# Where the sines and the products kn, qn stand in a four-block cycle of attention under an MLP

## The chip, the cores and the metric

One core of a Trainium2 chip runs the whole program. The number is device microseconds of one execution, from the first to the last instruction and what the launch puts around them; lower is better. The engines are named as in the profile: PE (TensorE, the matrix engine), PEld (its weight loads), ACT (ScalarE, functions from tables), DVE (VectorE, elementwise), POOL (GpSimd), SP (SyncE, which here only issues DMAs).

## What is computed

A linear attention with a complex decay, followed by two MLP layers:

```python
for t in range(S):                       # S = 768, 4 batches, 8 heads, 48 wide
    S_re, S_im = ar * S_re - ai * S_im + kv, ar * S_im + ai * S_re
    y[:, :, t] = q[:, :, t] @ S_re       # (ar, ai): a_re, a_im scaled to at most 0.999
x = y as 3072 tokens of 384
h = x @ w_in;  x = (h - tanh(h)) @ w_out       # d_ff = 2048
h = x @ w_in2; x = (max(h, 0) ** 2) @ w_out2
```

The kernel uses no loop over t. The time axis is cut into 6 chunks of 128 steps; in a chunk, logarithms of the magnitudes and angles of a are summed by a triangular matmul, exponentials and sines of the sums turn q and k, and the decay becomes an ordinary masked product of the turned q and k.

## The kernel before

The MLP sets the pace. It is cut into blocks: one block is one group of 512 tokens and one slice of 128 of the 2048 hidden columns, with nine matmuls h (first weight, three k-slices with three products each of a number split in high and low halves) and nine matmuls acc (second weight). 17 blocks make the first group, 16 every other; there are 6 groups and 2 layers. The acc of a block stand two blocks behind its h. Between them ACT makes t = tanh(h), DVE the difference h - t, ACT the high half gh, DVE the low half gl (`act_parts`, line 284).

Attention is cut into units, 4 batches in each of 6 chunks; unit n has chunk c = n // 4 and batch b = n % 4. A unit is a list of steps 0 to 15 (lines 790 to 817), and each step is done in one block, four blocks apart from the same step of the next unit. So four units are in flight, and every fourth block is a visit: there stand step 15 of one unit, 11 of the next, 7 of the third, 3 of the fourth. From the second group on, while attention lasts, `chain["on"]` is true and every engine works in the order in which the code is written (class `Turn`, line 144); before and behind that a scheduler orders the instructions. In a block, the second number of a step is its key: keys are sorted, and `block_step` (line 1066) cuts them at 1.35, 1.75, 5, 6 and 7 to put the parts of the MLP between them. Keys under 5 stand before the block's h matmuls, the others behind them.

The steps in question, for a unit of chunk 2 or later:

- a0 loads ri (a_re, a_im, in three rotating buffers), a1 squares it on ACT into ab.
- a2 takes logarithms and exponentials (one table), a3 works on them on DVE, a3b splits ab into lh and ll.
- a6l sums on PE into pc, a7x takes the exponentials of pc into ee (the table of a2). a4 is the arctangent, a5c and a5s work on its result, a6 sums into pu, a7 makes the fraction of a turn in fg and sends its last row to DRAM (crow) for the next chunk.
- a8 takes the two sines of fg in place, a9 multiplies q and k by them into kn and qn (two DVE instructions each), t0 and t1 turn these over on PE into pk and pq, ACT copies them to kqT.
- In step 15: strips, pU, px on PE, wm on DVE; a12v copies px into the next group's tokens (xh, xl), a13v updates the state.

Functions of ACT come from tables, and `table(...)` (line 166) writes a load where the set in force lacks the function: logarithms and exponentials need one set, the arctangent a second (sigmoid), the sine a third (silu); tanh is in the second and the third. `ready(...)` is such a load ahead of time. PSUM has one bank for h in this part (`ps_tile`, line 86), so the next h waits until DVE has made h - t; pU, pu and pk share a second, px, pc and pq a third.

At a group's end `put_x2` (line 328) copies the three acc banks through tiles x2t to DRAM. The tag x2t has two buffers; with `third` the third copy takes a tile of another pool.

Of the kernel before, what the change touches and what calls it, by code (L numbers as in the profile page):

```python
# [43 lines left out]
def kernel(  # L44
# [10 lines left out]
    B, S, HV, DP = v.shape  # L55
# [86 lines left out]
    chain = {"on": False}  # L142
# [23 lines left out]
    def table(*names):  # L166
        if act_set["name"] not in names and not general[0]:
            name = names[0]
            with ExitStack() as es:
                for o in act_set["ops"] or [act_set["load"]]:  # L170
                    if o is not None:
                        es.enter_context(tc.issue_after(o))
                load = act_e.preload_act_table_set(name).ins
            act_set.update(name=name, load=load, ops=[])
# [138 lines left out]
    def g2(layer, m, g, acc, cs=slice(0, TG), js=range(KD)):  # L313
        gh, gl = g
        wh, wl = (w_[:, DM:] for w_ in wts[layer, m])
        first = m <= 0 and cs.start == 0
        end = m in (-1, NM - 1)
        for j in js:
            sl = slice(j * P, (j + 1) * P)
            o = acc[j][:, cs]  # L320
            ten.matmul(o, wh[:, sl], gh, start=first, stop=False)
            ten.matmul(o, wh[:, sl], gl, start=False, stop=False)
            ten.matmul(o, wl[:, sl], gh, start=False, stop=end)

    def new_acc():
        return [ps_c.tile([P, TG], F32, tag="c", name="acc") for _ in range(KD)]

    def put_x2(acc, dst, third=False):
        for j in range(KD):
            if third and j == 2:  # L330
                t = spool.tile([P, n2], F32, tag="cv", name="x2t")[:, :TG]
            else:
                t = gpool.tile([P, TG], F32, tag="x2t", name="x2t", bufs=2)
            if j % 2 == 0:
                act_e.copy(t, acc[j])
            else:
                dve.tensor_copy(t, acc[j])
            sp.dma_start(dst(j), t)
# [18 lines left out]
    def put_out(ap3, acc, g, j, cs=slice(0, TG), vector=False):  # L357
        t = ap3.tile([P, TG], F32, tag="ot", name="ot", bufs=3)
        if vector:
            dve.tensor_copy(t[:, cs], acc[j][:, cs])  # L360
        else:
            act_e.copy(t[:, cs], acc[j][:, cs])
        sp.dma_start(out[g, j * P:(j + 1) * P, cs], t[:, cs])
# [16 lines left out]
    at = [xpool.tile([P, 2, HH, P], F32, tag=g, name=f"at_{g}") for g in ("xh", "xl")]  # L380
# [16 lines left out]
    def unit(n):  # L397
        c, b = divmod(n, B)
# [225 lines left out]
        def a10(i):  # L624
            def pe():
                for src, nm in ((V["kn"], "pk"), (V["qn"], "pq")):
                    pt = bank(nm)
                    w = P if packed else D2
                    nt = n2 // w // 2
                    for j in range(nt):  # L630
                        ten.transpose(
                            pt[:w, j * P:(j + 1) * P],
                            src[:, (i * nt + j) * w:(i * nt + j + 1) * w], ident,
                        )
                    V[nm, i] = pt

            def ev():
                for dst, nm in (("kT", "pk"), ("qT", "pq")):
                    w, nt = (P, 3) if packed else (D2, HH)
                    act_e.copy(  # L640
                        T(dst, i)[:w, :nt].rearrange("p j t -> p (j t)"),
                        V[nm, i][:w, :nt * P],
                    )
                if packed:
                    for j in range(3):
                        sp.dma_start(
                            kqT[i][32 * j:32 * j + 32, :, 3, :], kqT[i][D2:P, :, j, :]
                        )

            return pe, ev  # L650

        def a11(half=range(2)):
            for i in half:
                sc = bank("sc").rearrange("p (j t) -> p j t", j=HH)
                for j in range(HH):
                    ten.matmul(
                        sc[:, j, :], head("kT", i * HH + j), head("qT", i * HH + j),
                        start=True, stop=True,
                    )
                V["sc", i] = sc  # L660
# [4 lines left out]
        def a11s(i):  # L665
            sc = strips[i]
            for j in (0, 2, 1, 3):
                h = i * HH + j
                for s in range(4):
                    g = 3 - s if turned(h) else s  # L670
                    ten.matmul(
                        sc[32 * g:32 * g + 32, j, 32 * s:],
                        head("kT", h)[:, 32 * s:32 * s + 32],
                        head("qT", h)[:, 32 * s:], start=True, stop=True,
                    )

        def a11m(i):
            sc = strips[i]
            wm = ap1.tile([P, HH, P], F32, tag=f"wm{i}", name=f"wm{i}_{n}")
            dve.tensor_tensor(  # L680
                wm.rearrange("p (a j) t -> p a j t", a=2),
                sc.rearrange("p (a j) t -> p a j t", a=2),
                maskab.unsqueeze(2).to_broadcast([P, 2, HH // 2, P]), op=ALU.mult,
            )
            V["wm", i] = wm
# [90 lines left out]
        t0, t0v = a10(0)  # L776
        t1_, t1v = a10(1)
        if c == 0:
# [3 lines left out]
                t0=t0, e0=t0v, t1=t1_, e1=t1v, s0=lambda: a11((0,)), s1=lambda: a11((1,)),  # L782
                m0=lambda: a11v((0,)), m1=lambda: a11v((1,)),
                px=a12, x=a12v, pU=a13, st=a13v, ff=fill,
            )
        def ready(name):
            if chain["on"]:
                table(name)

        if not packed:  # L790
            return [
                (i, dict(p=1, e=5.1, v=5.2, p2=6.1, v2=6.2)[kind], f) for i, kind, f in (
# [7 lines left out]
                )  # L800
            ]
        late = n - 2 * B
        ln = (2, 6.37) if late == 2 else (3, 1.4)
        ex = (6, 6.36) if late == 1 else (7, 1.3)
        at = (8, 6.05) if late == 1 else (7, 6.1)
        return [
            (0, 5.2, a0), (1, 5.2, a1), ln + (a2,), (3, 1.5, lambda: ready("sigmoid_and_others")),
            (4, 5.1, a3), (5, 5.1, a3b), (6, 6.3 if late < 2 else 1.1, a6l),
            (6, 1.4, a0c), ex + (a7x,), (7, 2.0, l2), at + (a4,), (at[0], 7.1, a5c),
            (8, 5.1, a7r), (9, 5.3, a5s), (9, 5.4, a8x),  # L810
            (10, 6.3 if late < 1 else 1.1, a6), (10, 6.4 if late < 1 else 1.2, a7),
            (10, 1.3, lambda: ready("silu_and_others")), (10, 6.5, a8),
            (11, 1.9, a9), (12, 5.2, l3), (12, 6.1, t0), (12, 6.2, t0v), (13, 6.1, t1_), (13, 6.2, t1v),
            (15, 1.1, lambda: a11s(0)), (15, 1.2, lambda: a11m(0)), (15, 1.5, a13),
            (15, 1.6, lambda: a11s(1)), (15, 1.7, lambda: a11m(1)), (15, 1.8, a12),
            (15, 2.1, a13v), (15, 2.2, a12v),
        ]

    NST = 16
# [1 line left out]
    for n in range(B, NU):  # L821
        c, b = divmod(n, B)
        s0 = (c - 1) * NM + 3 + 4 * b - (NST - 1)
        for i, key, f in unit(n):
            plan.setdefault(s0 + i, []).append((key, f))
# [175 lines left out]
    def x2_dst(g):  # L1001
        return lambda j: x2g[g][j]
# [6 lines left out]
    NB0 = len(blocks)  # L1009
# [7 lines left out]
    cur = {"g2": 0, "acc": None, "pool": gpool, "recheck": 0, "split": 0, "signs": 0}  # L1017
# [7 lines left out]
    def second_half(n):  # L1025
        l, g, m, cs = blocks[n]
        if m == 0 and cs.start == 0:
            cur["acc"] = new_acc()
        g2(l, m, gs.pop(n), cur["acc"], cs)
        if m == NM - 1:  # L1030
            if l == 0:
                put_x2(cur["acc"], x2_dst(g), third=chain["on"])
            else:
                for j in range(KD):
                    put_out(cur["pool"], cur["acc"], g, j, vector=j % 2 == 1)
# [30 lines left out]
    def block_step(t):  # L1066
# [46 lines left out]
        while cur["g2"] < NB and cur["g2"] <= t - (LAG if t >= NATT + 2 else 2):  # L1113
            second_half(cur["g2"])
            cur["g2"] += 1
# [22 lines left out]


    first = {f"{n}{k}": f for n in range(B) for k, f in unit(n).items()}  # L1140
    first.update(C=clear_pads, W=conv_ahead, J=conv_tick, B=lambda: block_step(0))
    for k in START.split():
# [101 lines left out]
```

## Time and profile before

| | us |
|---|---|
| three runs | 995.70, 996.23, 996.36 |
| median | 996.23 |
| the profiled execution | 995.56 |
| its span, first to last instruction | 993.6 |
| PE busy | 953.1 (96%) |
| ACT busy | 643.6 (65%) |
| DVE busy | 543.4 (55%) |
| attention under the MLP, chained | about 160 to 521 |
| MLP alone | about 521 to 993 |

The profiled execution is 0.67 under the median, and 1.96 of it lie outside the span. A busy PE is a share of time in which a matmul was under way; matmuls overlap, so a row's duration (0.39 for 512 columns) is longer than the distance to the next (about 0.23).

### The profile page before, as it was taken

To read this page: it belongs to the slowest core of one execution; us is meant where nothing else is said; L and a number is where in the kernel's file an instruction comes from. 1 tells how busy PE (TensorE), PEld (TensorE's weight loads), DVE (VectorE), ACT (ScalarE), POOL (GpSimd) and SP (SyncE) were. 2 spreads that over 40 slices of the span, in tenths; PEclk is the share of its full clock that TensorE was granted. 3 is DMA by queue.
4 is the path that set the end of the run, shared out by engine and by line. 5 is a ranking of instruction groups with operands and counts; after the bars stand their busy time and mean duration, and the time that the engine had idled before them with its cause. 6 is when DMAs were issued, how large, how long until landed. Compare 5 with 4: busy or idle time off the path is not lost.

```text
span 993.6 us, 18356 instructions
## 1 busy us (share of the span) xinstructions
PE 953.1 (96%) x7424; PEld 786.6 (79%) x7424; DVE 543.4 (55%) x902; ACT 643.6 (65%) x1133; POOL 19.3 (2%) x41
## 2 busy tenths in 40 slices
PE   3999997999999999999999998999999999999997
PEld 1888776888788888888888887888888888888886
DVE  5999986666666666665547995132222322322111
ACT  8789886777777777777634445455666565555442
POOL 2000000000000000000000010000000000000000
PEclk9999999999999999999999999999999999999999
DMA  7444522222222232122117543034353343320000
GB/s 264 133 136 152 174 59 77 70 58 57 90 58 69 64 116 62 59 60 74 41 34 265 187 159 127 0 114 157 112 191 117 122 154 132 127 96 32 32 1 34
DMA packets 56945, 101.01 MB, mean 102 GB/s; under 512 B 23172, under 2 KB 32664, under 8 KB 56856
## 3 DMA queue, kind: packets, MB, share of 16 engines
q1 hardware_dynamic: 56712, 99.67, 31.0%
q8 instruction: 59, 0.97, 0.4%
q14 instruction: 30, 0.25, 0.1%
q10 hardware_dynamic: 144, 0.13, 0.0%
HBM read 87.09 MB, written 9.47 MB: 97 GB/s over the span
## 4 chain that ended last, share of the span: by engine, by line
PE 71%; ACT 10%; issue 7%; DVE 7%; DMA 4%; SPq 1%; POOL 0%; ACTq 0%; POOLq 0%; DVEq 0%
PE h L155 31%; PE acc L155 30%; PE px L155 4%; ACT L155 3%; ACT ab L155 2%; DMA crow<-fg 1%; PE strips L155 1%; ACT ee L155 1%; PE pk L155 1%; ACT fg L155 1%; PE pq L155 1%; DMA ri<-in_ri_dram 1%; DVE cv L155 1%; PE pU L155 1%; ACT gh L155 1%
## 5 line engine op out<-in xcount | busy, mean ns | idle before, releaser
L155 DVE TENSOR_TENSOR gl<-t,gh 128x512 fp32r<-128x512 f32 (+1 forms) x193 | 132.5, 687 | 225.0 <-ACT gh L155 224.6
L155 ACT ACTIVATE t<-h 128x512 f32<-128x512 f32 (+1 forms) x193 | 114.8, 595 | 192.9 <-PE h L155 189.8
L155 PE MATMUL h<-xh,wh 128*128 128x512 f32 (+1 forms) x579 | 228.8, 395 | 3.3 <-DVE t L155 1.8
L155 PE MATMUL acc<-gh,wh 128*128 128x512 f32 (+1 forms) x579 | 228.3, 395 | 2.5 <-ACT x2t L155 2.5
L155 PE MATMUL h<-xl,wh 128*128 128x512 f32 (+1 forms) x579 | 225.8, 390 | 0.1
L155 PE MATMUL h<-xh,wl 128*128 128x512 f32 (+1 forms) x579 | 225.8, 390 | 0.0
L155 PE MATMUL acc<-gl,wh 128*128 128x512 f32 (+1 forms) x579 | 225.1, 389 | 0.0
L155 PE MATMUL acc<-gh,wl 128*128 128x512 f32 (+1 forms) x579 | 225.1, 389 | 0.0
L155 ACT CAST gh<-t 128x512 fp32r<-128x512 f32 (+1 forms) x193 | 119.4, 619 | 76.3 <-PE acc L155 41.5
L155 PEld LDWEIGHTS h<-xh,wh 128*128 128x128 f32 x579 | 108.9, 188 | 30.0 <-issue 3.6
L155 PEld LDWEIGHTS acc<-gh,wh 128*128 128x128 f32 x579 | 108.8, 188 | 24.4 <-ACT x2t L155 3.0
L155 PEld LDWEIGHTS h<-xh,wl 128*128 128x128 f32 x579 | 109.0, 188 | 22.9
L155 PEld LDWEIGHTS acc<-gh,wl 128*128 128x128 f32 x579 | 108.7, 188 | 22.6
L155 PEld LDWEIGHTS h<-xl,wh 128*128 128x128 f32 x579 | 109.0, 188 | 21.6 <-DVE xl L155 0.4
L155 PEld LDWEIGHTS acc<-gl,wh 128*128 128x128 f32 x579 | 108.9, 188 | 21.6 <-DVE gl L155 0.2
L155 DVE TENSOR_TENSOR t<-h,t 128x512 f32<-128x512 f32 (+1 forms) x97 | 66.1, 682 | 56.6 <-ACT t L155 55.9
L155 ACT ACT_TABLE_LOAD x67 | 86.0, 1283 | 1.8 <-PEq L1226 0.8
L155 ACT ACTIVATE t<-t 128x512 f32<-128x512 f32 x96 | 60.2, 627 | 1.7
L155 DVE TENSOR_TENSOR wmin<-wmin,cz 128x768 bf16<-128x768 bf16 x32 | 17.8, 558 | 57.4 <-ACT cz L155 57.4
L155 DVE TENSOR_TENSOR wm<-strips,maskab 128x512 f32<-128x512 f32 x32 | 21.8, 690 | 29.9 <-PE strips L155 29.9
L155 ACT ACTIVATE ab<-ri 128x768 f32<-128x768 f32 x24 | 20.3, 848 | 17.7 <-DVE ll L155 9.8
L155 DVE SCALAR_TENSOR_TENSOR jw<-st,jw 128x768 int32<-128x768 int32 x32 | 30.4, 951 | 0.2
(125 smaller groups left out, 983.2 us busy)
## 6 DMA issues: line engine op xcount, KB each, us to landing
st<-in_w_dram SPq DMA_DIRECT2D x32, 768.0 KB
sr<-in_w_dram SPq DMA_DIRECT2D x32, 768.0 KB
ri<-in_ri_dram SPq DMA_DIRECT2D x24, 384.0 KB
qk<-in_qk_dram SPq DMA_DIRECT2D x24, 384.0 KB
vz<-in_v_dram SPq DMA_DIRECT2D x16, 384.0 KB
x2d<-x2t SPq DMA_DIRECT2D x18, 256.0 KB
xf<-x2d SPq DMA_DIRECT2D x6, 768.0 KB
ss<-in_ri_dram SPq DMA_DIRECT2D x12, 384.0 KB
```

The lines of the kernel that those rows point to most:

```text
L155: r = op(*a, **kw)
```

## The change

The sines (a8) leave the visit's neighbour, step 10, and stand in step 11, in the visit, right behind the logarithms, with their table load ahead of them; the load of the sigmoid set that was written behind the logarithms goes, and the arctangent brings its own. kn and qn (a9) move in the visit from before h to behind it. So does a12v, save for a group's last unit. ri is loaded in step -1, not 0, so in the visit ahead of DVE's work of it; qk (l2) is loaded at key 6.2 instead of 2.0, behind a9. The third buffer of x2t is used for all blocks behind the first group's, not while the order is chained. For unit 8, `first`, the sines have key 2.3.

```diff
-        def ready(name):
-            if chain["on"]:
-                table(name)
...
         late = n - 2 * B
+        first = late == 0
...
-            (0, 5.2, a0), (1, 5.2, a1), ln + (a2,), (3, 1.5, lambda: ready("sigmoid_and_others")),
+            (-1, 2.05, a0), (1, 5.2, a1), ln + (a2,),
             (4, 5.1, a3), (5, 5.1, a3b), (6, 6.3 if late < 2 else 1.1, a6l),
-            (6, 1.4, a0c), ex + (a7x,), (7, 2.0, l2), at + (a4,), (at[0], 7.1, a5c),
+            (6, 1.4, a0c), ex + (a7x,), (7, 6.2, l2), at + (a4,), (at[0], 7.1, a5c),
             (8, 5.1, a7r), (9, 5.3, a5s), (9, 5.4, a8x),
-            (10, 6.3 if late < 1 else 1.1, a6), (10, 6.4 if late < 1 else 1.2, a7),
-            (10, 1.3, lambda: ready("silu_and_others")), (10, 6.5, a8),
-            (11, 1.9, a9), (12, 5.2, l3), (12, 6.1, t0), (12, 6.2, t0v), (13, 6.1, t1_), (13, 6.2, t1v),
+            (10, 6.3 if first else 1.1, a6), (10, 6.4 if first else 1.2, a7),
+            (11, 1.45, lambda: table("silu_and_others")), (11, 2.3 if first else 1.46, a8),
+            (11, 6.15, a9), (12, 5.2, l3), (12, 6.1, t0), (12, 6.2, t0v), (13, 6.1, t1_), (13, 6.2, t1v),
             (15, 1.1, lambda: a11s(0)), (15, 1.2, lambda: a11m(0)), (15, 1.5, a13),
             (15, 1.6, lambda: a11s(1)), (15, 1.7, lambda: a11m(1)), (15, 1.8, a12),
-            (15, 2.1, a13v), (15, 2.2, a12v),
+            (15, 2.1, a13v), (15, 2.2 if b == B - 1 else 6.05, a12v),
...
-                put_x2(cur["acc"], x2_dst(g), third=chain["on"])
+                put_x2(cur["acc"], x2_dst(g), third=n > NB0)
```

ACT in the visit of unit 9 (its step 15; step 11 of unit 10, 7 of unit 11, 3 of unit 12). The number behind a tile's name is its unit, the last one its buffer; ab and ri of unit 12 are the logarithms, ri of unit 11 the arctangent, fg of unit 10 the sines. Before:

```order
L155 ACTIVATE fg_10_2361<-fg_10_2361 128x384
L155 ACT_TABLE_LOAD
L155 ACTIVATE ee_11_2413<-pc_2358 128x384 x2
L155 CAST gh_2380<-t_2379 128x512
L155 ACTIVATE ab_12_2318<-ab_12_2318,b_tiny_105 128x384
L155 ACTIVATE ab_12_2318<-ab_12_2318 128x384 x2
L155 ACTIVATE ri_12_2273<-ab_12_2318,b_eps_107 128x384
L155 ACT_TABLE_LOAD
L155 ACTIVATE xh2_2222,chk_y_120<-px_2469 128x3x128
L155 ACTIVATE t_2524<-h_2514 128x512
L155 ACTIVATE ri_11_1966<-ri_11_1966 128x384
L155 CAST gh_2525<-t_2524 128x512
```

The same place now, from the high half behind ee on:

```order
L155 CAST gh_2379<-t_2378 128x512
L155 ACTIVATE ab_12_2318<-ab_12_2318,b_tiny_105 128x384
L155 ACTIVATE ab_12_2318<-ab_12_2318 128x384 x2
L155 ACTIVATE ri_12_2211<-ab_12_2318,b_eps_107 128x384
L155 ACT_TABLE_LOAD
L155 ACTIVATE fg_10_2361<-fg_10_2361,b_hpi_111 128x384
L155 ACTIVATE fg_10_2361<-fg_10_2361 128x384
L155 ACTIVATE t_2515<-h_2505 128x512
L155 ACTIVATE xh2_2230,chk_y_120<-px_2468 128x3x128
L155 ACT_TABLE_LOAD
L155 ACTIVATE ri_11_1909<-ri_11_1909 128x384
L155 CAST gh_2516<-t_2515 128x512
```

The sines have come in behind the logarithms with a load ahead of them; xh and a third load now stand between the tanh of the visit and its gh.

DVE at the same place, from qn of unit 10 (kn stands right ahead) to t, the difference h - tanh(h), of the block behind the visit. Before:

```order
L155 TENSOR_TENSOR qn_10_2505<-qk_10_2218,fg_10_2361 128x6x96
L155 TENSOR_TENSOR qn_10_2505<-qk_10_2218,fg_10_2361 128x6x32
L155 TENSOR_TENSOR state1_130<-state1_130,pU_2424 96x8x48
L155 TENSOR_TENSOR state1_130<-state1_130,rall_121 96x8x48
L155 TENSOR_TENSOR xl2_2223<-px_2469,xh2_2222 128x3x128
L155 TENSOR_TENSOR t_2524<-h_2514,t_2524 128x512
L155 SCALAR_TENSOR_TENSOR ri_11_1966<-cr11_2367,ri_11_1966 1x384
L155 TENSOR_TENSOR gl_2526<-t_2524,gh_2525 128x512
L155 TENSOR_TENSOR ri_12_2273<-ri_12_2273,ab_12_2318 128x384
L155 SCALAR_TENSOR_TENSOR ab_12_2318<-ab_12_2318,ri_12_2273 128x384
L155 TENSOR_TENSOR t_2563<-h_2542,t_2563 128x512
```

Now, from t of the visit on:

```order
L155 TENSOR_TENSOR t_2515<-h_2505,t_2515 128x512
L155 TENSOR_TENSOR xl2_2231<-px_2468,xh2_2230 128x3x128
L155 TENSOR_TENSOR kn_10_2524<-qk_10_2242,fg_10_2361 128x6x96
L155 TENSOR_TENSOR kn_10_2524<-qk_10_2242,fg_10_2361 128x6x32
L155 TENSOR_TENSOR qn_10_2527<-qk_10_2242,fg_10_2361 128x6x96
L155 TENSOR_TENSOR qn_10_2527<-qk_10_2242,fg_10_2361 128x6x32
L155 SCALAR_TENSOR_TENSOR ri_11_1909<-cr11_2366,ri_11_1909 1x384
L155 TENSOR_TENSOR gl_2517<-t_2515,gh_2516 128x512
L155 TENSOR_TENSOR ri_12_2211<-ri_12_2211,ab_12_2318 128x384
L155 SCALAR_TENSOR_TENSOR ab_12_2318<-ab_12_2318,ri_12_2211 128x384
L155 TENSOR_TENSOR t_2563<-h_2544,t_2563 128x512
```

kn and qn have moved from ahead of the visit's t to between it and the next block's t.

SP where the chain begins, before:

```order
L155 DMA qk_8_1709<-in_qk_dram 128x768
L155 DMA er9_1839<-ee_9_1835 1x384
L155 DMA crow_128<-fg_8_1845 1x16x24
L155 DMA qk_9_1917<-in_qk_dram 128x768
L155 DMA rall_121<-er9_1839 16x8x1 x6
L155 DMA vz_133<-in_v_dram 128x768
L155 DMA ri_11_1966<-in_ri_dram 128x768
L155 DMA kqT0_134<-kqT0_134 32x2x128 x3
```

And now:

```order
L155 DMA qk_8_1717<-in_qk_dram 128x768
L155 DMA ri_11_1909<-in_ri_dram 128x768
L155 DMA er9_1839<-ee_9_1835 1x384
L155 DMA crow_128<-fg_8_1845 1x16x24
L155 DMA qk_9_1923<-in_qk_dram 128x768
L155 DMA rall_121<-er9_1839 16x8x1 x6
L155 DMA vz_133<-in_v_dram 128x768
L155 DMA kqT0_134<-kqT0_134 32x2x128 x3
```

The load of ri for unit 11 stood behind qk of unit 9 and all that waits with it; it stands ahead of them now.

## Rows read from the trace of the kernel before

**Rows 1.** Waits over the span: engine, tile, releaser, us in total, times, longest.

```profile
PE px L155 <- ACT ee L155: 4.5, 6, 1.0
...
ACT fg L155 <- DMA crow<-fg: 4.7, 5, 1.1
```

**Rows 2.** Busy time of four whole cycles: stretch, its length, PE, PEld, DVE, ACT, POOL, clock.

```profile
249.83:273.29 23.46, 22.59 (x265) 18.93 (x265) 15.08 (x28) 17.22 (x32) 0.00 (x0) 1.00 0.31 95
273.29:296.86 23.57, 22.56 (x266) 18.92 (x265) 14.96 (x28) 17.11 (x31) 0.00 (x0) 1.00 0.23 61
...
341.62:364.90 23.28, 22.59 (x266) 18.93 (x265) 15.80 (x30) 17.99 (x33) 0.00 (x0) 1.00 0.31 95
...
387.24:409.62 22.38, 22.38 (x265) 18.86 (x265) 14.70 (x28) 17.00 (x31) 0.00 (x0) 1.00 0.23 64
```

**Rows 3.** Timeline of ACT in an undisturbed visit: start, us, instruction.

```profile
403.92 0.60 ACT L155 ACTIVATE t<-h 128x512 f32<-128x512 f32 x1 [0.56 <-PE h L155]
...
405.44 1.28 ACT L155 ACT_TABLE_LOAD   x1
406.74 0.87 ACT L155 ACTIVATE ee<-pc 128x384 f32<-128x384 f32 x2
...
409.98 1.28 ACT L155 ACT_TABLE_LOAD   x1
...
411.94 0.60 ACT L155 ACTIVATE t<-h 128x512 f32<-128x512 f32 x1
```

**Rows 4.** Timeline of DVE in the same visit and the next block.

```profile
409.15 1.02 DVE L155 TENSOR_TENSOR kn<-qk,fg 128x576 f32<-128x576 f32 x2
410.08 1.02 DVE L155 TENSOR_TENSOR qn<-qk,fg 128x576 f32<-128x576 f32 x2
...
412.07 0.55 DVE L155 TENSOR_TENSOR xl<-px,xh 128x384 fp32r<-128x384 f32 x1
412.57 0.69 DVE L155 TENSOR_TENSOR t<-h,t 128x512 f32<-128x512 f32 x1
413.18 0.54 DVE L155 SCALAR_TENSOR_TENSOR ri<-cr,ri 1x384 f32<-1x384 f32 x1
...
416.65 0.69 DVE L155 TENSOR_TENSOR t<-h,t 128x512 f32<-128x512 f32 x1 [1.08 <-ACT t L155]
```

**Rows 5.** Timeline of PE and SP behind the same visit.

```profile
413.78 0.39 PE L155 MATMUL h<-xh,wh 128*128 128x512 f32 x1
...
415.83 0.49 PE L155 MATMUL pk<-ident,kn 128*128 128x128 f32 x3
...
417.40 6.65 SPq L155 DMA_DIRECT2D kqT<-kqT  x6
...
418.56 0.39 PE L155 MATMUL h<-xh,wh 128*128 128x512 f32 x1
```

**Rows 6.** Timelines of DVE, ACT and PE where the chain begins.

```profile
163.36 0.53 DVE L155 TENSOR_TENSOR ll<-ab,lh 128x384 fp32r<-128x384 f32 x1
...
167.03 0.84 ACT L155 ACTIVATE ab<-ri 128x768 f32<-128x768 f32 x1 [4.70 <-DMA ri<-in_ri_dram]
...
169.73 0.68 DVE L155 TENSOR_TENSOR t<-h,t 128x512 f32<-128x512 f32 x1
...
169.19 0.69 PE L155 MATMUL pu<-th,tri 128*128 128x384 f32 x1 [2.63 <-ACT kqT L155]
```

**Rows 7.** Busy time of the 2.1 us behind that, columns as in rows 2.

```profile
170.60:172.70 2.10, 2.10 (x6) 1.69 (x6) 1.25 (x3) 2.08 (x5) 0.00 (x0) 0.52 0.30 73
```

**Rows 8.** Timelines of ACT and PE at the copies x2t of two later groups.

```profile
530.21 0.59 ACT L155 COPY x2t<-acc 128x512 f32<-128x512 f32 x1
...
534.11 0.59 ACT L155 COPY x2t<-acc 128x512 f32<-128x512 f32 x1 [2.60 <-DMA x2d<-x2t]
...
607.30 0.50 PE L155 MATMUL acc<-gh,wh 128*128 128x512 f32 x1 [2.55 <-ACT x2t L155]
```

**Rows 9.** Timeline of PE before the chain.

```profile
104.47 0.50 PE L155 MATMUL h<-xh,wh 128*128 128x512 f32 x1 [1.18 <-DVE t L155]
```

## The prediction

> **What bounds the kernel now.** I read the views in this order: the waits over the whole span, the stretches of the attention part one cycle at a time, then the rows of ACT, DVE and PE in one cycle, and last the two places where PE stands still for over 2 us.
>
> From about 180 to 519 us the kernel repeats a cycle of four blocks, one of which is a visit (the PE work of one attention unit stands in it). In an undisturbed cycle PE is busy for all of its 22.38 us, while DVE has 14.70 and ACT 17.00 [rows 2]. So PE is the bound, and nothing that ACT or DVE saves can shorten such a cycle. What can go is the time in which PE waits. Six visits make the px matmuls wait for ee, 4.5 us of idle PE in all, 1.0 at most; five times a sine waits for the DMA of crow, 4.7 in all [rows 1]. Both belong together: px and pc share a PSUM bank, the exponentials (ee) have to read pc out of it first, and they stand on ACT behind two sines and a table load. Outside the cycle there are two long stops: 2.63 at pu, behind ACT's square of ri, which waited 4.70 for the load of ri [rows 6], and 2.55 at acc behind the third copy x2t, in the first blocks of the second layer [rows 8].
>
> **The change part by part.** Call the visit's block v, its neighbours v-1 and v+1.
>
> *ACT in the visit.* The number of table loads stays three in a cycle; their places move. Before, v-1 had one, v two; now all three are in v. The rows [rows 3]: tanh of v-1 at 403.92, 1.52 later the load at 405.44 (0.50 for the tanh, 1.02 for two sines); ee from 406.74; next load at 409.98, 4.54 after the first. Now the first load starts at the tanh's end, 404.52, so ee ends at 406.7 instead of 407.6: 0.92 sooner in every visit, and by the crow wait more where there was one. The second load comes at 404.52 + 4.54 = 409.06, the sines end at 409.06 + 1.30 + 1.02 = 411.38. The tanh of v waits for its h and starts at 411.94: 0.56 of cover. Behind it follow xh, the third load (1.28), arctan, gh: gh at about 414.9 to 415.5, and the acc that reads it comes two blocks later, so this costs nothing.
>
> Every load in these rows is 1.28 long and the next instruction starts 0.02 behind it [rows 3]. The Trainium skill says otherwise (ScalarE: Activation LUTs, What ACT_TABLE_LOAD costs): it gives about 2.66 us for each switch of sets, 1.28 of load and 1.38 of drain. The load agrees with the trace, a drain of that size does not show here; by the page ACT would be 2.8 us later at the tanh of v, and it is the rival below.
>
> *What that takes away.* The cycles at 249.83, 273.29 and 341.62 last 23.46, 23.57 and 23.28 against 22.38 [rows 2], 3.2 us in sum, each with a px wait. The two in the last group I put at 0.5 each, an estimate from the 4.5 less four of 0.9. There the visit lacks pU, so PE reaches the tanh of v sooner and I give 0.3 back. Sum 3.9.
>
> *kn and qn on DVE.* These four instructions (two of 1.02 per pair) stood at 409.15 to 411.10, before t of v; now they stand between xl and gl of v, ahead of t of v+1 [rows 4]. Counted with the start-to-start times of these rows: t of v at 412.57, xl 413.18, kn 413.65, qn 414.58, the cr row 415.51, gl 416.05, 0.61 on two instructions of a3 (0.47 each, like xl), t of v+1 at 417.6, ending at 418.3. PE starts pk at 415.83 and pq behind it, for which kn and qn are there at 414.6 and 415.6; and it starts h of v+2 at 418.56 [rows 5], which needs the one h bank that t frees. Cover 0.25. It was 1.2, as t ended at 417.34. With whole durations instead (0.69 + 0.55 + 1.02 + 1.02 + 0.54 + 0.69 + 0.55 + 0.55 + 0.69 = 6.30, gl as t, a3 as xl) t would end at 418.87 and PE wait 0.31 a visit. DVE rows that follow each other in these rows start before the one ahead ends, so I take the first: 0. It is the thinnest cover of the change. Block v+2 starts some 0.6 us late on ACT and DVE, and since v+3 has lost its table load of 1.28, the cycle catches up.
>
> *qk, ri and SP.* The load of qk now waits on SP for qn, so until 415.6. Behind it stand rall, vz and kqT. The kqT copies ran from 417.40 to 424.05 [rows 5], and the strips that read them come with the next visit, a cycle of 22.38 behind the load at 405.44: three us of cover for a delay of two. The load of ri no longer stands behind these.
>
> *The first cycle.* Here ri matters [rows 6]. ACT's square of ri ran at 167.03; without the wait it needs only ll, so 163.36 + 0.53 = 163.9, 3.1 sooner. Then pu finds its operands, and the idle 2.63 goes. In the 2.10 us from 170.60 the granted clock is 0.52, the level of 1.2 GHz, after PE had stood still, and six matmuls take 2.10 instead of 1.36 [rows 7]: 0.7 more, and I estimate as much for the four sums ahead of them. The px wait of this visit (about 0.9) goes too. Sum 4.9. Late next is t of that block: 170.41 - 3.1 = 167.3, where PE arrives at 167.2, so 0.1 back.
>
> *The third x2t buffer.* It now applies from the second group on, not while the order is chained. In the first group (around 168) the third copy then has to reuse the first one's buffer. The nearest rows are 530.21 and 534.11, copy to copy 3.90 with the DMA between [rows 8]. First copy at 167.9, third at 171.8 to 172.4; acc wants the bank at 170.8: 1.6 lost, and ACT behind it makes ee late, 0.5. Bounds: 0 (the bank is needed later) to 3.9. So the first cycle gains 4.9 - 0.1 - 2.1 = 2.7. In the last group of the first layer the change is the other way: the wait of 2.55 [rows 8] has a buffer of its own now, and the row order puts acc of that bank ahead of the next h. Late next is gl of the block two later, about level with PE. I take 2.5, bounds 2.0 to 2.7.
>
> *Before the chain.* Up to 155 us a scheduler orders the code; moved rows of ri shift px and pk by a few matmuls and one DVE conversion behind a t. The stop nearest to this is 1.18 of PE waiting for t [rows 9]; I bound the effect by 1.2 either way and take 0.
>
> **Sum.** 3.9 + 2.7 + 2.5 = 9.1 us. The profiled execution took 995.56 (993.6 of span, 2.0 around it); 995.56 - 9.1 = 986.5. It lay 0.67 under the median of 996.23, so on the median's scale 987.1.
>
> **Rivals.**
> 1. *DVE is the next wait.* With whole durations h of v+2 waits 0.35 in some 13 visits: 4.6 lost, 991.7. For it: the cover is 0.25 on a queue of nine instructions. Against: the start-to-start rows.
> 2. *Not ee.* If px in fact waits for something else of PE's own, the 3.9 and the 0.9 stay: 991.9. Against: the longer cycles are just those with a crow wait or an ACT copy ahead.
> 3. *Better than forecast.* The x2t copy is not waited for and the start gains its 1.2: 987.1 - 2.1 - 1.2 = 983.8.
> 4. *Slower: ACT fills the visit.* Three loads in one block and all of a visit's functions stand ahead of the tanh of v. If the two loads in front of it cost more by x together, the tanh is late by x - 0.56 and h of v+1 by x - 1.08 (its bank has 0.52 of cover: t ended at 413.26 [rows 4], h started at 413.78 [rows 5]). In 13 visits this eats the whole gain from x = 1.08 + 9.1 / 13 = 1.8. With one load's length more for each, x = 2.56: 13 x 1.48 = 19.2 lost, 1006.3. Against: no load of these rows takes more than 1.28. With the 1.38 of drain that the Trainium skill's page (ScalarE: Activation LUTs, What ACT_TABLE_LOAD costs) adds to a load, the same sum gives an estimate of 13 x 1.68 = 21.8 and 1008.9; no row here shows such a drain, so it changes no chance.
> 5. *It does nothing that counts.* The gains at the two stops are given back by the order before the chain and by DVE: within 2 us of 996.2.
>
> **How the numbers follow.** Forecast 0.57 (by itself 984.5 to 990), rival 1 0.15, rival 2 0.07, rival 3 0.09, rival 4 0.06, rival 5 0.06. Range 982.5 to 992: it takes in the forecast and rivals 1 to 3 with their bounds, and leaves out rivals 4 and 5 and a little of the rest. A measurement of this kernel can tell about 0.2% from no change, 2 us: faster by more than that 0.88, within it 0.06, slower 0.06.
>
> **What would show it.** Right: no px wait for ee left, undisturbed cycles still at 22.4, pu without its stop and the clock at 1.0 there, a short stop at the first acc around 171 behind x2t, none around 605, sines behind the ri exponential in each visit. Wrong: PE waiting for DVE t at h two blocks behind each visit (rival 1), PE waiting at h one block behind it with ACT's load or sine as the last (rival 4), px still idle with ee long done (rival 2).

## The result and the profile after

The changed kernel takes 984.88 us (median of 4, 983.86 to 985.54) beside 996.30 for the kernel before, ratio 0.9884, 95% interval 0.9867 to 0.9901: 11.4 us faster. The forecast was 987.1, in a range of 982.5 to 992.0. The profiled execution has a span of 982.7 where before it was 993.6, so 10.9 of the gain can be followed in the traces. The page begins:

```profile
span 982.7 us, 18400 instructions
## 1 busy us (share of the span) xinstructions
PE 952.4 (97%) x7424; PEld 785.7 (80%) x7424; DVE 539.8 (55%) x902; ACT 641.5 (65%) x1133; POOL 19.1 (2%) x41
```

PE is as busy as before; what went is idle time. To see where, set the start of the same h row in both traces side by side. Blocks are counted from 0; a difference that grows between two rows was gained or lost between them.

| first h of block | before | after | difference |
|---|---|---|---|
| 0 | 53.53 | 54.54 | +1.0 |
| 18, the chain's second block | 161.64 | 162.73 | +1.1 |
| 20, behind the first chained visit | 180.65 | 177.51 | -3.1 |
| 80, behind the last visit | 518.98 | 511.07 | -7.9 |
| 102, in the second layer | 609.70 | 598.95 | -10.75 |

So: 1.1 lost up to there, 4.2 gained in the first cycle, 4.8 in the visits, 2.85 at the end of the first layer.

Waits over the span of the changed kernel (engine, tile, releaser, total, times, longest), against [rows 1]: the six px waits for ee, 4.5 in all, are one of 0.3, and the five waits of a sine for crow are one, in block 17.

```profile
ACT x2t L155 <- DMA x2d<-x2t: 2.3, 1, 2.3
...
PE px L155 <- issue: 1.0, 3, 0.4
...
ACT fg L155 <- DMA crow<-fg: 0.9, 1, 0.9
...
PE acc L155 <- ACT x2t L155: 0.3, 1, 0.3
...
PE px L155 <- ACT ee L155: 0.3, 1, 0.3
```

The same four cycles as in [rows 2], busy time by stretch. The three that had lasted 23.3 to 23.6 are now like the undisturbed one:

```profile
246.77:269.10 22.33, 22.33 (x267) 18.85 (x264) 14.58 (x28) 17.06 (x33) 0.00 (x0) 1.00 0.34 100
269.10:291.43 22.33, 22.33 (x269) 18.84 (x265) 14.50 (x28) 16.79 (x31) 0.00 (x0) 1.00 0.26 64
336.08:358.41 22.33, 22.33 (x269) 18.84 (x265) 15.29 (x29) 17.79 (x33) 0.00 (x0) 1.00 0.35 99
380.74:403.06 22.32, 22.32 (x268) 18.83 (x264) 14.49 (x28) 16.78 (x31) 0.00 (x0) 1.00 0.24 64
```

By cover I mean how much later a piece of work could end before another engine waits for it. ACT in an undisturbed visit, to be read against [rows 3]: the load ahead of ee follows the tanh at once (398.07 behind 397.45), and the sines end at 404.92, 0.51 ahead of the visit's tanh.

```profile
397.45 0.60 ACT L155 ACTIVATE t<-h 128x512 f32<-128x512 f32 x1 [1.68 <-PE h L155]
398.07 1.28 ACT L155 ACT_TABLE_LOAD   x1
399.36 0.87 ACT L155 ACTIVATE ee<-pc 128x384 f32<-128x384 f32 x2
...
402.59 1.28 ACT L155 ACT_TABLE_LOAD   x1
...
404.41 0.51 ACT L155 ACTIVATE fg<-fg 128x384 f32<-128x384 f32 x1
405.43 0.60 ACT L155 ACTIVATE t<-h 128x512 f32<-128x512 f32 x1 [0.52 <-PE h L155]
```

DVE and PE there, against [rows 4, 5]. The second t ends at 411.02 + 0.67 = 411.69, and PE starts the h that needs its bank at 412.03: 0.34 of cover. The first t ends at 406.75, 0.52 ahead of the h at 407.27.

```profile
406.06 0.69 DVE L155 TENSOR_TENSOR t<-h,t 128x512 f32<-128x512 f32 x1 [2.25 <-ACT t L155]
...
408.07 1.02 DVE L155 TENSOR_TENSOR qn<-qk,fg 128x576 f32<-128x576 f32 x2
...
411.02 0.67 DVE L155 TENSOR_TENSOR t<-h,t 128x512 f32<-128x512 f32 x1
```

```profile
407.27 0.39 PE L155 MATMUL h<-xh,wh 128*128 128x512 f32 x1
...
412.03 0.39 PE L155 MATMUL h<-xh,wh 128*128 128x512 f32 x1
```

The first cycle, ACT and then PE, against [rows 6]: the square of ri no longer waits for its load, pu comes without a stop, and the third copy x2t waits 2.28 on ACT, of which PE feels 0.32 at acc and 0.27 at px.

```profile
165.01 0.84 ACT L155 ACTIVATE ab<-ri 128x768 f32<-128x768 f32 x1 [1.59 <-DVE ll L155]
...
168.96 0.58 ACT L155 COPY x2t<-acc 128x512 f32<-128x512 f32 x1
171.83 0.59 ACT L155 COPY x2t<-acc 128x512 f32<-128x512 f32 x1 [2.28 <-DMA x2d<-x2t]
```

```profile
167.51 0.34 PE L155 MATMUL pu<-th,tri 128*128 128x384 f32 x1
...
172.47 0.50 PE L155 MATMUL acc<-gh,wh 128*128 128x512 f32 x1 [0.32 <-ACT x2t L155]
...
175.62 1.08 PE L155 MATMUL px<-kqT,state 96*32 96x128 f32 x32 [0.27 <-ACT ee L155]
```

### The profile page after: what moved, and what is told of

It reads as the page before. It is cut to its first block, busy times and chain, and to the rows that moved or that the text cites. A ratio compares the mean times of both kernels' runs of the same rounds, so it can differ in the third digit from the quotient of the medians.

```text
span 982.7 us, 18400 instructions
## 1 busy us (share of the span) xinstructions
PE 952.4 (97%) x7424; PEld 785.7 (80%) x7424; DVE 539.8 (55%) x902; ACT 641.5 (65%) x1133; POOL 19.1 (2%) x41
## 4 chain that ended last, share of the span: by engine, by line
PE 85%; ACT 8%; DVE 3%; DMA 2%; issue 1%; SPq 0%; ACTq 0%; DVEq 0%
PE h L155 37%; PE acc L155 37%; PE px L155 4%; ACT L155 2%; PE strips L155 2%; ACT ab L155 2%; PE pk L155 1%; PE pq L155 1%; PE pU L155 1%; PE pu L155 1%; ACT ee L155 1%; ACT fg L155 1%; DMA ri<-in_ri_dram 1%; DVE cv L155 1%; ACT ri L155 1%
## 5 line engine op out<-in xcount | busy, mean ns | idle before, releaser
L155 DVE SCALAR_TENSOR_TENSOR cv<-st,cv 128x768 int32<-128x768 int32 x32 | 30.3, 950 | 0.1
```

The lines of the kernel that those rows point to most:

```text
L155: r = op(*a, **kw)
```

## The experiments

In these runs the kernel before had medians of 997.9 to 998.0 (single runs 995.5 to 1000.6), so ratios are compared: the changed kernel has 0.9884. The changed kernel was not run beside them, so what differs from it by a us or two is read from the traces.

**The moves without the early ri.** From the changed kernel:

```diff
-            (-1, 2.05, a0), (1, 5.2, a1), ln + (a2,),
+            (0, 5.2, a0), (1, 5.2, a1), ln + (a2,),
-                put_x2(cur["acc"], x2_dst(g), third=n > NB0)
+                put_x2(cur["acc"], x2_dst(g), third=chain["on"])
```

> Only the moves of the sines, of kn and qn, of a12v and of the load of qk; ri is loaded in step 0 as before, and the third x2t buffer is used as before. If the parts add up, the visits gain what they gain in the changed kernel (4.8 us between the 20th and the 80th block), the first cycle gains only its px wait (0.9), and the stops of 2.6 at pu and 2.5 behind x2t stay: 5.7 us, 996.3 to 990.6. The rival is that the moves need the earlier ri: the load of ri would stand on SP behind that of qk, which now waits for qn, ACT's square of ri would come late in every cycle, and PE would wait at pu; then the visits gain less than 2 us and the kernel ends at 994 or later.

Measured 1038.22, ratio 1.0399 (1.0382 to 1.0417): 40 us slower than the kernel before. The rival was right in its mechanism and far too small. SP, ACT and PE of one cycle:

```profile
372.70 0.34 SPq L155 DMA_DIRECT2D qk<-in_qk_dram  x1
373.14 2.74 SPq L155 DMA_DIRECT2D rall<-er  x6
375.92 0.44 SPq L155 DMA_DIRECT2D vz<-in_v_dram  x1
376.40 1.80 SPq L155 DMA_DIRECT2D ri<-in_ri_dram  x1
```

```profile
381.18 0.84 ACT L155 ACTIVATE ab<-ri 128x768 f32<-128x768 f32 x1 [4.84 <-DMA ri<-in_ri_dram]
```

```profile
383.34 0.44 PE L155 MATMUL pu<-th,tri 128*128 128x384 f32 x1 [2.31 <-ACT kqT L155]
```

SP works in order. The load of qk waits for qn, which here ends 3.2 behind the start of the visit's tanh where it ended 0.8 ahead of it [rows 3, 4]; the six issues of rall take 2.74 and ri comes last. Its square starts 4.8 behind the issue, and the sums of that step wait. In the kernel before, up to the last group, the square stood 3.8 to 5.2 behind the issue, behind the first chained visit always waiting for ll alone:

```profile
346.84 0.43 SPq L155 DMA_DIRECT2D ri<-in_ri_dram  x1
...
351.24 0.85 ACT L155 ACTIVATE ab<-ri 128x768 f32<-128x768 f32 x1 [0.82 <-DVE ll L155]
```

In the moves alone it starts 4.0 to 4.8 behind it (5.7 in the last cycle), waiting for the load each time. So next to nothing was to spare. Behind the first chained visit there are eleven such stops at pu, 0.9 to 3.9 long, 25.1 in all. The rest of the 41.7 lost between blocks 20 and 80 is mostly slow matmuls: in the 6 us behind the stop at 383.34 the granted clock is 0.72 (a part at 1.0, a part at 0.5, which is 1.2 GHz), and from block 20 to 80 its mean is 0.96 where the kernel before has 1.00.

```profile
383.34:389.34 6.00, 5.71 (x18) 4.33 (x19) 3.64 (x7) 3.23 (x7) 0.00 (x0) 0.72 0.44 149
```

**The same with ri ahead of rall.** One key is changed in the kernel just shown:

```diff
-            (0, 5.2, a0), (1, 5.2, a1), ln + (a2,),
+            (0, 5.05, a0), (1, 5.2, a1), ln + (a2,),
```

> The kernel of the moves alone (1038.2), with ri's load put ahead of rall's six DMAs and vz in SP's order, still behind the load of qk. In the trace of the moves alone SP issues qk at 372.70, rall from 373.14 to 375.88, vz, and ri only at 376.40; the square of ri starts 4.8 behind that and PE stops 2.3 at pu. Theory: ri's place in the queue is the cause, 3.2 sooner takes away the stops of the cycles with rall (27 us with the low clock behind them), 1008 or less; the last group's cycles have no rall and keep theirs. The rival: the wait of SP for qn ahead of qk decides, and rall is not what ri waits for; then the stops stay at 2 us and the time at 1030 or more.

Measured 992.03, ratio 0.9934 (0.9910 to 0.9958): 46 us from the place of six DMA issues of 0.46 each and of vz. The theory holds, though its number was too high: the last group's stops are nearly gone too (0.20 and 0.28 stay). There ri went out 4.86 and 0.86 behind qk in the moves alone, and goes out 0.41 and 0.40 behind it here; the first of the two does have rall, against the expectation. In the rows ri goes out right behind qk, and its square waits only for ll:

```profile
342.09 0.37 SPq L155 DMA_DIRECT2D qk<-in_qk_dram  x1
342.51 0.41 SPq L155 DMA_DIRECT2D ri<-in_ri_dram  x1
343.01 2.75 SPq L155 DMA_DIRECT2D rall<-er  x6
```

```profile
346.54 0.85 ACT L155 ACTIVATE ab<-ri 128x768 f32<-128x768 f32 x1 [0.82 <-DVE ll L155]
```

**The early ri alone**, in the kernel before:

```diff
-            (0, 5.2, a0), (1, 5.2, a1), ln + (a2,), (3, 1.5, lambda: ready("sigmoid_and_others")),
+            (-1, 2.05, a0), (1, 5.2, a1), ln + (a2,), (3, 1.5, lambda: ready("sigmoid_and_others")),
```

> The kernel before with ri loaded one block sooner, nothing else. My theory: ri alone ends the stop of 2.63 at pu and the stretch of low clock behind it (1.4), so h of the 20th block starts 4.0 sooner and nothing later changes; the px wait of that visit (0.97) stays, as do the five later ones: 996.3 to 992.3. The rival: the square of ri is not what held pu, or the time is given back at the visit behind it (px waits 0.97 plus what was gained): less than 1.5 us gained, 995 or later.

Measured 996.15, ratio 0.9982 (0.9968 to 0.9996): 1.8 us, not 4.0. The stop at pu is gone and h of block 19 starts 3.3 sooner, but PE then waits for ee, which still stands behind a sine that waits for crow, and the px row runs at the slow clock (1.79 for 32 matmuls, 1.08 otherwise). So in the first cycle the early ri alone is not enough: most of what it gains is lost again at ee.

```profile
176.18 1.79 PE L155 MATMUL px<-kqT,state 96*32 96x128 f32 x32 [2.08 <-ACT ee L155]
```

**Is it the DMA of crow or the place of the sines?** In the kernel before, the tile fg gets a third part; the sine of F goes there, so the row that crow's DMA reads is not overwritten:

```diff
+            elif name == "fg":
+                t = pool.tile([P, 3 * HD], F32, tag=name, name=f"{name}_{n}")
+                if packed:
+                    V["F"], V["cs"], V["G"] = t[:, :HD], t[:, HD:], t[:, n2:]
+                    return t
+                t = t[:, :n2]
...
-            V["cs"] = V["ab"] if c == 0 else V["fg"]
+            if not packed:
+                V["cs"] = V["ab"] if c == 0 else V["fg"]
```

> The kernel before, but the first of the two sines' inputs is kept: its sine is written to a third part of the tile, so that it need not wait until the DMA of crow has read the last row. Nothing is moved. Theory: of the six px waits the four with a crow wait ahead (0.97, 0.87, 1.01, 0.69) are the DMA's, and go without any move, the two in the last group (0.47 each) stay: 3.5 gained, 992.8. The rival: it is the place of two sines and a load ahead of ee that makes px wait; then all six waits stay at 0.4 or more and less than 1 us is gained.

Measured 992.02, ratio 0.9932 (0.9913 to 0.9951): 6.8 us, twice what was expected. The px waits at blocks 36, 40 and 52 are gone and give 1.07, 1.18 and 0.89, nearly as much as in the changed kernel (1.08, 1.21, 0.91). The two of 0.47 in the last group stay, as expected; so does the one in the first visit (0.81), against the expectation. So three of the six waits were the DMA's, and for these the sines could have stayed. Another 1.7 of the trace's gain lies up to block 20, most of it at pu: around block 17 the sine waited for crow too, hence kn, qn and, on SP, the load of qk; now qk goes out at 157.31 instead of 159.15, ri at 161.02 instead of 162.87, and the stop of 2.63 is gone. A part is lost again in block 17, where h waits 1.49 for xl, which DVE now makes behind kn and qn. It is the same queue as in the moves alone, from its other end.

One stop got dearer. The wait behind x2t is 2.77 here (2.55 before), and h of block 102 and 103 lose 5.9 there, not 2.85: behind it the clock is at 0.50 for 6 us, while in the trace of before it stays at 1.00. So this trace gains 5.65 up to block 80 and only 2.7 over the span; of the four runs the fastest, 989.53, has the highest mean clock, 0.999. Busy time by stretch (columns as in [rows 2], the clock third from the end), this kernel and then the kernel before:

```profile
601.80:607.80 6.00, 5.93 (x14) 4.68 (x15) 4.29 (x6) 3.12 (x6) 0.00 (x0) 0.50 0.12 44
```

```profile
607.30:611.00 3.70, 3.70 (x16) 3.08 (x17) 3.40 (x5) 2.96 (x5) 0.00 (x0) 1.00 0.19 71
```

**The x2t buffer.** Alone in the kernel before (`third=n > NB0`), and in the changed kernel for all groups (`third=True`):

> The kernel before with the third x2t buffer for all groups behind the first, nothing else. Theory: the stop of 2.55 at acc in the first blocks of the second layer goes, 2.85 as in the changed kernel; at the first group's end the third copy now waits for the first one's DMA, which costs 0.5 to 1.0 there: 2 us gained, 994.3. The rival is my own forecast of that wait, 2.1: then 0.7 gained, 995.6.

> The changed kernel with the third x2t buffer for every group, the first too. In the changed kernel's trace the third copy of the first group waits 2.28 on ACT, and PE loses 0.3 at acc and 0.3 at px behind it. Theory: both go, h of the 20th block starts 0.7 sooner, 984.2 where the changed kernel has 984.9. The rival: ACT only gets to ee sooner and PE then waits for the next thing there, nothing gained; my forecast of 2.1 for that copy would give 982.8.

Alone: 995.75, ratio 0.9974 (0.9964 to 0.9983), 2.6 us. Block 102 gains 2.85 as in the changed kernel, the first cycle loses 1.2, a little over the expected 0.5 to 1.0: the third copy starts 2.85 behind the first, and fg, the sines and ee behind it make px wait 2.64 where it waited 0.97.

```profile
171.76 0.58 ACT L155 COPY x2t<-acc 128x512 f32<-128x512 f32 x1
174.61 0.58 ACT L155 COPY x2t<-acc 128x512 f32<-128x512 f32 x1 [2.27 <-DMA x2d<-x2t]
```

For all groups: 984.53, ratio 0.9861 (0.9844 to 0.9878). In the trace the waits at acc and px are gone, and blocks 17 to 20 take 0.6 less than in the changed kernel (0.7 expected); by the time alone it can't be told from it.

**How thick are the covers?** Five edits of the changed kernel, each to one row of the unit's list. One or two more loads of a table that nothing uses, ahead of the sines:

```diff
+            (11, 1.44, lambda: chain["on"] and table("sigmoid_and_others")),
             (11, 1.45, lambda: table("silu_and_others")), (11, 2.3 if first else 1.46, a8),
```

> The changed kernel with one more table load ahead of the sines in 14 visits (it loads a set that nothing uses). In the changed trace the sines end 0.51 ahead of the visit's tanh and its t ends 0.52 ahead of the next h. Theory: these two covers add, a load of 1.28 costs 0.25 a visit, 3.5 us, 988.4. The rivals: it is hidden wholly, 985; or a load costs more than its row shows, 1.38 of drain beside it (the figure of the Trainium skill, ScalarE: Activation LUTs, What ACT_TABLE_LOAD costs), which by the same covers would be 1.63 a visit, an estimate of 22.8 and 1007.7.

> The same with two more loads in each of the 14 visits. Theory: 2 x 1.28 less the two covers of 1.03 is 1.53 a visit, 21.4 us, 1006. If the first is hidden and the second costs a whole load, 18 us, 1003; if nothing is hidden, 36 us, 1021.

One more: 992.01, ratio 0.9935 (0.9917 to 0.9953). Two more: 1010.50, ratio 1.0128 (1.0105 to 1.0150). From block 20 to block 80 the traces lose 8.0 and 24.0. The visit of one more load, ACT and PE, then that of two:

```profile
407.35 2.57 ACT L155 ACT_TABLE_LOAD   x2
```

```profile
412.23 0.50 PE L155 MATMUL h<-xh,wh 128*128 128x512 f32 x1
```

```profile
419.47 3.86 ACT L155 ACT_TABLE_LOAD   x3
```

```profile
425.63 0.50 PE L155 MATMUL h<-xh,wh 128*128 128x512 f32 x1 [1.32 <-DVE t L155]
```

Two loads take 2.57 and three 3.86, that is 1.29 each. At h behind an undisturbed visit the first costs 0.19 and both cost 1.48: the two covers (0.51 and 0.52) add and are worth 1.03, as expected, and beyond them a load costs its own length. What was not expected are 0.17 and 0.14 more in the two blocks behind each stop, without a wait that the profile names; 0.11 of each stand at the block's first matmul (the last section). More is lost where the cover is thinner: for one load 1.1 in the first visit and 0.7 to 0.8 at blocks 49, 65 and 69. That is why one load lost 8.0 and not 3.5; 0.8 of the 8.0 are pauses that have other lengths here (the last section). The figure of 1.38 of drain with every switch of sets (the Trainium skill, ScalarE: Activation LUTs, What ACT_TABLE_LOAD costs) does not show here: the second extra load would have cost 2.66 and cost 1.29.

kn and qn ahead of the visit's h, as before, the sines left in their new place (`(11, 2.35 if first else 1.9, a9)`):

> The changed kernel, but kn and qn stand ahead of the visit's h again, as before, while the sines stay behind the logarithms. Theory: the sines end at 404.92 in the undisturbed visit of the changed trace; kn, qn and the two instructions on the state behind them put the end of t of the visit at 408.6, where the next h wants its bank at 407.27: 1.3 a visit, 17 us in 13 visits, 1002. The rival: the visit's DVE has room (t waits 2.25 for ACT there), nothing lost, 985.

Measured 1004.54, ratio 1.0061 (1.0043 to 1.0079): slower than the kernel before. PE waits 1.18 for t at the next h, and an undisturbed cycle loses 1.34 and then 0.16; 1.3 was expected.

```profile
420.48 1.03 DVE L155 TENSOR_TENSOR kn<-qk,fg 128x576 f32<-128x576 f32 x2 [2.19 <-ACT fg L155]
...
423.42 0.68 DVE L155 TENSOR_TENSOR t<-h,t 128x512 f32<-128x512 f32 x1
```

```profile
424.15 0.50 PE L155 MATMUL h<-xh,wh 128*128 128x512 f32 x1 [1.18 <-DVE t L155]
```

Two more DVE instructions behind qn (`dve.tensor_tensor(t, V["qn"][:, :HD], V["qn"][:, HD:], op=ALU.add)`, twice, at key 6.16 of step 11):

> The changed kernel with two more DVE instructions of 128x384 (0.47 each in a row) behind kn and qn; their result is not used. In the changed trace t of the block behind the visit ends at 411.69 and h of the next starts at 412.03: 0.34 of cover. Theory: 0.94 less 0.34 is 0.6 of wait a visit, and some 0.15 behind it as in the runs with more loads, 13 to 14 visits, 10 us, 995. The rival by whole durations (0.55 each and no cover) gives 1.1 a visit or more, 1000; if DVE has more room than the rows show, 985 to 988.

Measured 998.25, ratio 1.0000 (0.9988 to 1.0012), 3 us more than expected. They take 1.18 and not 0.94: from t to t it is now 422.79 - 416.65 = 6.14, and it was 4.96. The second writes the tile of the first, which may be why; no run tests it. 1.18 less the cover of 0.34 is 0.84; h two blocks behind the visit lost 0.89, and the next block 0.14. The cover is what the starts of the rows say.

```profile
419.71 1.15 DVE L155 TENSOR_TENSOR spend<-qn 128x384 f32<-128x384 f32 x2
...
422.79 0.67 DVE L155 TENSOR_TENSOR t<-h,t 128x512 f32<-128x512 f32 x1
```

```profile
423.51 0.50 PE L155 MATMUL h<-xh,wh 128*128 128x512 f32 x1 [0.73 <-DVE t L155]
```

a12v ahead of h for every unit (`(15, 2.2, a12v)`):

> The changed kernel with a12v ahead of the visit's h for every unit, as before: ACT copies px to xh ahead of the tanh, DVE makes xl ahead of t. In the changed trace the tanh would start at about 405.5 where it starts at 405.43, and t would end at 406.8 where the next h wants its bank at 407.27. Theory: covered, no loss, 985. The rival: xh and xl take their 0.5 from the same cover that the extra load showed (visits behind a group's last unit, which have this order, lost 0.5 more there), and the visits lose 0.2 to 0.5, 988 to 991.

Measured 985.36, ratio 0.9872 (0.9849 to 0.9896), no loss that can be told; in the trace block 20 to 80 took 0.75 longer, 0.41 of it in the first visit's block and the next, where PE waits 0.10 for t, and 0.14 in pauses that are not its own (the last section). So by itself this part of the change gains little; it keeps cover: in the run of one more load, of the visits from block 36 to 64, the two that have this order in either kernel, ahead of blocks 49 and 65, lost 0.66 each where the others lost 0.19.

**A faster version.** The x2t buffer for all groups and the three-part fg, both in the changed kernel:

> The kernel with the third x2t buffer for every group, and the sine of fg written to a part of its own, so that the visit of the 17th block need not wait for the DMA of crow (0.89 there in the changed trace, with PE waiting 0.38 and 0.33 for kn and qn behind it). Theory: those go, h of the 18th block starts 0.7 sooner, and later cycles have no crow wait to lose: 983.8. The rival: behind kn and qn something else of that block is late (xl, which the 17th block's h waits for), nothing gained, 984.5.

Measured 983.39, ratio 0.9853 (0.9830 to 0.9875), the fastest of all. In the trace it gains 1.2 on the changed kernel between blocks 17 and 80, 1.0 of it between blocks 17 and 18, where kn and qn come sooner. By the time alone the two intervals overlap.

## Why the prediction was right, and where its terms were off

- **Visits: forecast 3.9, measured 4.8.** The three long cycles gave 3.20 of 3.2. The two of the last group gave 0.70 and 0.68, where 0.5 each less 0.3 was forecast. That term is the step that failed: the 0.3 was not given back, and the 0.5 is the wait as the profile counts it (0.47), while each of the five px waits cost 0.20 to 0.23 more than was counted. The last 0.2 are quiet cycles, a little shorter than before. The cause given was half the truth: ee did come sooner in every visit, but in the three long cycles it was enough to be rid of the wait for crow, as the run with fg in three parts shows. Only the two of the last group needed the move: these two waits stay in the kernels that leave the sines in place, and are gone with ri ahead of rall, where the sines are moved.
- **First cycle: forecast 2.7, measured 4.2.** The step that failed is the price of the third copy, 2.1; it cost 0.6, with both bounds (0 to 3.9) around it. Two things in it were off. The time from copy to copy was taken from [rows 8], 3.90, a stretch in which weights are loaded; here it was 2.87. And the bank was said to be wanted at the block's first acc: the waiting acc is the block's seventh of nine, 1.4 later. The 4.9 ahead of it held to within 0.1, but not as a sum of parts: ri alone brought a third of it.
- **End of the first layer: forecast 2.5 (2.0 to 2.7), measured 2.85.** The step from the wait to its cost failed: h behind it came 0.3 later than the wait of 2.55 alone explains. The rows have 0.16 of it ahead of the wait that is counted and 0.11 at the first matmul behind it (the last section).
- **Before the chain: forecast 0 within 1.2, profiled +1.1.** It is nearly all there at block 0 (+1.0). In the traces of all kernels block 0 starts between 53.4 and 54.9, on whichever kernel they are built; the times of before and after differ by 11.4, more than the 10.9 of the traces. I take it for scatter of single executions; no run was made for it alone.
- **DVE, rival 1: did not come.** Start-to-start times gave 0.25 of cover, the trace shows 0.34 and the run with more DVE work confirms it. Whole durations would have put a wait into every cycle (0.31 by the rows of the prediction, 418.87 - 418.56; the 0.35 of its rival is a slip).
- **ACT, rival 4: did not come.** Covers of 0.56 and 0.52 were forecast, 0.51 and 0.52 are there, and the extra loads spend them as the sum said.
- **What was missed.** The prediction saw that SP's queue would be later behind qk and that ri "no longer stands behind these", and put no price on it, since ri was counted only where the trace of before showed a wait, in the first cycle. It was the condition of the whole: without it the same moves cost 40 us. The cover of ri in every other cycle was thin, and no wait in the trace of before pointed at it.

The signs named for a right forecast are in the trace, save that one px wait for ee of 0.3 is left, behind the third copy. Against the forecast of 9.1 the rows show 1.5 more gained in the first cycle, 0.9 in the visits and 0.35 at the end of the first layer, and 1.1 less before the chain: 10.75 at block 102. The medians differ by 11.4; the 0.5 by which that is more than the 10.9 of the spans stands in no row.

## What to carry to other kernels

When a step moves later, follow what its last reader holds up on an in-order DMA queue: here one load that waits for a product took six small issues and another load with it, and a trace without a wait there said nothing of how near it was. Take the length of a DMA wait from a stretch with the same traffic, and find the very matmul that needs the bank, not the first of its row. Price a stop by the starts of the rows around it, not by the wait that is counted. Before an operation is moved to get out of a wait, see whether the wait is for a copy that an extra piece of tile would free.

## What had not been expected of the hardware

- Stops of nearly one length had different prices. At the same acc behind x2t, the clock stayed at 1.00 behind 2.55 (the kernel before) and 2.85 were lost; behind 2.50 (ri ahead of rall) it was 0.51 from 601.94 to 604.90 and 4.2 were lost; behind 2.77 (fg in three parts) it was 0.50 for 6 us and 5.9 were lost. At another place, in the run of ri alone px ran slow behind 2.08.
- A stop costs more than the wait that the profile counts. It counts from the end of the row ahead, 0.39 behind that row's start, where the next matmul would have started after 0.23: 0.16 come on top. So a wait of 1.18 cost 1.34, one of 1.32 cost 1.48 and one of 0.73 cost 0.89. The first matmul behind a stop then stands 0.34 ahead of the next instead of 0.23: this is 0.11 of the 0.11 to 0.19 more that the next block or two lose, in all four runs that put a stop into each cycle. The rest was not followed up.
- In three visits in a row the px matmuls pause for 0.2 to 1.0 with nothing to wait for. In the changed kernel 1, 11 and 22 of the last 32 are left at the pause, and the same numbers stand in the runs with more loads, with more DVE work and in the fastest version; in those built on the kernel before, and with kn and qn ahead, 9 or 10 and 19 are left in the second and third. In the moves alone 1, 12 and 22 are left, although the third pause comes 16 us later there. So the pause keeps a place in PE's program and not in time. What it is stays open; the three cycles it falls in last some 0.7 longer than others.
